# Attention and mixture of experts in one kernel: the tail keys' value product made full-height and rounded

## The chip, the cores and the metric

The kernel runs on one core of a Trainium2 chip. The time is that of one execution on the device, in microseconds (us); before the change it was 874.48 us, the median of three runs (874.23 to 874.96). Smaller is better.

## What is computed

```python
def _attn_ref(q, k, v):                       # 8 x 8 x 576 x 64
    scores = scale * np.matmul(q, k.transpose(0, 1, 3, 2))
    mask = block_i >= block_j                 # blocks of 64 positions
    scores = np.where(mask, scores, -1000000000.0)
    scores = scores - np.max(scores, axis=-1, keepdims=True)
    attn = np.exp(scores)
    attn = attn / (np.sum(attn, axis=-1, keepdims=True) + 1e-09)
    return np.matmul(attn, v)
...
def _moe_ref(x, modality_id, w_gate, modality_bias, w1, w2):   # 4608 x 512, 8 experts
    logits = x @ w_gate + modality_bias[modality_id]
    e_idx = np.argmax(logits, axis=1)
    ...
        h = np.maximum(x[mask] @ w1[e], 0.0)
        out[mask] = gate_w[mask, None] * (h @ w2[e])
```

Attention with a block-causal mask over 64 heads of 576 positions; then each position goes through one of eight experts. The change concerns the last step of the attention, the product of the exponentials with the values, for the last 64 keys and the last 64 queries of each head (576 is four chunks of 128 and a tail of 64).

## The kernel before

**Numbers as head and remainder.** Most products are made from rounded float32 (float32r, fp32r in the profile). A value is split into a rounded head, made by ScalarE (ACT), and a remainder, made by a subtraction on VectorE (DVE) or GpSimd (POOL), which is stored rounded as well. The values of a pair of heads stand in the tile vhl, 8 blocks of 128 keys, with head and remainder side by side as 128 weight columns (64 + 64); the exponentials, transposed, stand in two tiles, pth (heads) and ptl (remainders). A value product is a pair of matmuls with the same weights, one on pth, one on ptl. The output has 128 rows, of which the next product (back, L397) adds the two halves.

**The tail before the change.** The 64 x 64 block of the last keys and last queries goes another way: TensorE transposes the exponentials into 64 rows (L324), ACT copies them to p4 as unrounded float32 (copies, L341), and TensorE multiplies them with the unrounded values in vrt, weights of 64 x 64 (L380, issued at L383). The profile shows an unrounded product as two passes. It is the last product of part "Y", four 320-column ones being ahead of it, and it adds into 64 columns of the accumulator o1 of its head. Part "W", later, adds the other four products into the same accumulator: key chunk 3's (256 columns, two), then key chunk 2's (320 columns, two). "X" fills the first half of the output in another bank.

**The order of the work.** There are 32 pairs of heads. A slot (run_slot, L654) runs the steps of the table ORDER (L49): those with stage 0 for the slot's own pair, those with stage 1 for the pair before. Names: S scores, M maxima, E exponentials, T transposes, C copies to the rounded head (ACT), D remainders (DVE, rests), X, Y, W the value products, x, y their evacuation, K and Z the product back and the output rows; A and B are the two heads, q stands for a step of the routing of an earlier batch. The tail's block is transposed in TA1 and evacuated in CA1 and DA1, late in a pair's own slot; the products YA, WA, YB and WB follow in the next slot. "vh" (split_v) splits the pair's values early in its slot. At a slot's start the inputs of later pairs are loaded (load, L162; load_v, L226) and the next pair's keys and queries are split by POOL (split_qk, L198: L202, L203, L205, L207), with copies inside the chip between partition halves on SP's queue (L196, k2t; L206, z).

**Queues.** Engines TensorE, ACT, DVE and POOL take their work in the program's order throughout. SyncE (SP), which issues most transfers, does so in the first four slots only (L704 to L715); from then on the planner places SP's transfers by its own estimate of when each is ready, and each is then issued in the order it was placed, waiting for its data. The exponentials' four buffers, two pairs by two parts, and the value tiles alternate from pair to pair; vrt has three buffers and is reloaded (L229) when its readers, TensorE's product of the tail among them, are done.

After the attention, from about 440 us, the experts run (class Experts); they share the engines and reuse the buffers of the attention, and nothing of the change stands in them.

Of the kernel before, what the change touches and what calls it, by code (L numbers as in the profile page):

```python
# [11 lines left out]
F32 = mybir.dt.float32  # L12
F32R = mybir.dt.float32r
# [3 lines left out]
ALU = mybir.AluOpType  # L17
# [7 lines left out]
NPAIR = B * H // 2  # L25
# [67 lines left out]
def attention_moe(ctx, tc, qk, vr, bkw, mid, mb, w1, w2, cf, ci, cm, ld, out):  # L93
    nc = tc.nc
    pe, act, dve, pool = nc.tensor, nc.scalar, nc.vector, nc.gpsimd
# [8 lines left out]
    for n, shape in PARTS:  # L104
        size = int(np.prod(shape))
        v = cft[:, off : off + size]
# [21 lines left out]
    att = att_stack.enter_context(tc.tile_pool(name="att", bufs=2, side="right"))  # L128
# [30 lines left out]
    pairs = [Pair() for _ in range(NPAIR)]  # L159
# [66 lines left out]
    def load_v(p):  # L226
        d = pairs[p]
        d.vr = att.tile([128, 640], F32, name="vrt", bufs=3)
        nc.sync.dma_start(d.vr, vr[p])  # L229
        d.v = att.tile([128, 8, 2, 64], F32R, name="vhl", bufs=2)  # L230

    def split_v(p):
        d = pairs[p]
        v8 = d.vr[:, 0:512].rearrange("p (a b) -> p a b", a=8)
        act.copy(d.v[:, :, 0], v8)
        pool.tensor_tensor(d.v[:, :, 1], v8, d.v[:, :, 0], ALU.subtract)

    def scores(p, u):
        d = pairs[p]
# [52 lines left out]
    def row(j):  # L292
        return ROW0 + ROWS[j] * STEP

    def transposes(p, u):
        d = pairs[p]
        t = ps_t.tile([128, 512], F32, name="t")
        ev = []
        if u == "tl":
            for j in range(4):  # L300
                r = ROWS[j]
                pe.transpose(t[:, 128 * r : 128 * r + 128], d.ptail[:, 128 * j : 128 * j + 128], idf)
            src = t.rearrange("p (r h c) -> p h r c", r=4, h=2)
            ev.append((src, [x[:, :, ROW0 : ROW0 + 4 * STEP].rearrange("p h (r c) -> p h r c", r=4)[:, :, :, 256:320] for x in d.pt]))
            d.copies[u] = ev
            return
        h = "AB".index(u[0])
        pm = d.pm[h]

        def blk(c, j):  # L310
            o = CHUNK_OFF[c] + 128 * j
            return pm[:, o : o + 128]

        if u[1] == "0":
            for i, c in enumerate((2, 3, 0, 1)):
                pe.transpose(t[:, 128 * i : 128 * i + 128], blk(c, 0), idf)  # L316
            src = t.rearrange("p (a b) -> p a b", a=2)
            ev.append((src, [two(x, h) for x in d.pt]))
        elif u[1] == "1":
            for i, c in enumerate((1, 2, 3)):  # L320
                pe.transpose(t[:, 128 * i : 128 * i + 128], blk(c, 1), idf)
            ev.append((t[:, 0:384], [x[:, h, 128:512] for x in d.pt]))
            if h == 0:
                pe.transpose(t[0:64, 384:512], d.ptail[:, 512:576], idf)  # L324
                d.p4 = att.tile([64, 128], F32, name="p4", bufs=3)
                ev.append((t[0:64, 384:512], [d.p4]))
        else:
            for i, c in enumerate((2, 3)):
                pe.transpose(t[:, 128 * i : 128 * i + 128], blk(c, 2), idf)
            pe.transpose(t[:, 256:384], blk(3, 3), idf)  # L330
            ev.append((t[:, 0:256], [x[:, h, row(2) : row(2) + 256] for x in d.pt]))
            ev.append((t[:, 256:384], [x[:, h, row(3) + 128 : row(3) + 256] for x in d.pt]))
        d.copies[u] = ev

    def two(x, h):
        v = x[:, h, row(0) - 64 : X0 + 256]
        return v.rearrange("p (a b) -> p a b", a=2)[:, :, 64:320]
# [4 lines left out]

    def rests(p, u):
        for s, dst in pairs[p].copies[u]:
            if len(dst) > 1:
                dve.tensor_tensor(dst[1], s, dst[0], ALU.subtract)  # L346

    def sums(p):
        d = pairs[p]
# [11 lines left out]
    def values(p, h, part):  # L361
        d = pairs[p]
        if part == "X":
            d.o[h, 0] = o0
        if part == "Y":
            d.o[h, 1] = ps_o.tile([128, 512], F32, name="o1")
        mm = []
        for j in range(4):
            for x in d.pt:
                w = d.v[:, 4 * h + j].rearrange("p a b -> p (a b)")  # L370
                if part == "X":
                    if j < 2:
                        a = X0 if j == 0 else 0
                        mm.append((d.o[h, 0][:, 0:256], w, x[:, h, a : a + 256]))
                elif j < 3:
                    mm.append((d.o[h, 1][:, 0:320], w, x[:, h, row(j) : row(j) + 320]))
                else:
                    mm.append((d.o[h, 1][:, 64:320], w, x[:, h, row(j) + 64 : row(j) + 320]))
        if part != "X":
            last = (d.o[h, 1][0:64, 256:320], d.vr[0:64, 512 + 64 * h : 576 + 64 * h], d.p4[:, 64 * h : 64 * h + 64])  # L380
            mm = mm[0:4] + [last] if part == "Y" else mm[6:8] + mm[4:6]
        for i, (o, w, r) in enumerate(mm):
            pe.matmul(o, w, r, start=part != "W" and i == 0, stop=part != "Y" and i == len(mm) - 1)  # L383

# [629 lines left out]
def _constants():  # L1014
    p, j = np.indices((128, 128))
    late = np.arange(128) < 64
    ranks = np.broadcast_to(np.arange(NE) - NE, (128, 5, NE))
    seen = ranks.copy()
    seen[late, 4] = 100
    inv = np.zeros((128, 5))  # L1020
    inv[late, 4] = BIG
    first = np.ones((128, NE, 5))
    first[:, :, 0] = 0
    con = dict(
        idf=p == j,
        ii=p % 64 == j % 64,
        hm=p[:, 0:2] // 64 == j[:, 0:2],
        iom8=ranks[:, 0],
        iom40=ranks,
        iov40=seen,  # L1030
        inv5=inv,
        first5=first,
        base8=np.broadcast_to(np.arange(NE) * REGION, (128, NE)),
        edges=np.broadcast_to(np.arange(N // SLOT) * SLOT, (128, N // SLOT)),
    )
    cf = np.concatenate([con[n].reshape(128, -1) for n, _ in PARTS], axis=1).astype(np.float32)
    at = np.array([0, 128, 256, 384, 448])
    ci = (np.arange(B)[:, None] * S + at)[:, None] + np.arange(128)[None, :, None]
    ci = np.repeat(ci[..., None], IW, axis=3)
    cm = np.zeros((4, 2176), np.float32)  # L1040
    for r in range(4):
        cm[r, 0:1024].reshape(2, 512)[:] = (np.arange(512) >= 128 * r) & (np.arange(512) < 128 * r + 64)
        cm[r, 1024:2176].reshape(2, S)[:] = np.where((np.arange(S) >= 128 * r + 64) & (np.arange(S) < 128 * r + 128), FAR, 0)
    return dict(cf=cf, ci=ci.reshape(B, 128, 5 * IW).astype(np.int32), cm=cm, ld=np.where(j <= p, -1, 0).astype(np.float32))


def _prepare(q, k, v, moe_modality_id, moe_w_gate, moe_modality_bias, moe_w1, moe_w2):
    qt = q.reshape(NPAIR, 2, S, D).transpose(0, 1, 3, 2)
    kt = k.reshape(NPAIR, 2, S, D).transpose(0, 1, 3, 2)
    vp = v.reshape(NPAIR, 2, S, D)  # L1050
    qp = np.zeros((NPAIR, D, 2, 640), q.dtype)
    qp[:, :, 0, 0:576] = qt[:, 0]
    qp[:, :, 1, 0:512] = qt[:, 1, :, 0:512]
    qp[:, :, 1, 576:640] = qt[:, 1, :, 512:576]
    kp = kt.transpose(0, 2, 1, 3).reshape(NPAIR, D, 2 * S)
    qp = qp.reshape(NPAIR, D, 1280)
    one = np.concatenate([qp, kp], axis=2)
    qk = np.concatenate([np.concatenate([one, qp[:, :, 640 * h + 512 : 640 * h + 640]], axis=2) for h in range(2)], axis=1)
    vr = np.zeros((NPAIR, 128, 640), v.dtype)
    vr[:, :, 0:512] = vp[:, :, 0:512].reshape(NPAIR, 2, 4, 128, D).transpose(0, 3, 1, 2, 4).reshape(NPAIR, 128, 512)  # L1060
    vr[:, 0:64, 512:640] = vp[:, :, 512:576].transpose(0, 2, 1, 3).reshape(NPAIR, 64, 128)
    g = moe_w_gate.reshape(H, D, NE).transpose(1, 0, 2)
    bkw = np.zeros((2, D, PPB, 80), moe_w_gate.dtype)
    bkw[:, :, :, 0:8] = g[:, 0::2]
    bkw[:, :, :, 8:72] = np.eye(D)[:, None, :]
    bkw[:, :, :, 72:80] = g[:, 1::2]
    ids = moe_modality_id.reshape(B, S)
    mid = np.zeros((128, B, 5), ids.dtype)
    mid[:, :, 0:4] = ids[:, 0:512].reshape(B, 4, 128).transpose(2, 0, 1)
    mid[:, :, 4] = np.tile(ids[:, 512:576].transpose(1, 0), (2, 1))  # L1070
    mb = np.broadcast_to(moe_modality_bias.reshape(1, 2 * NE), (128, 2 * NE))
    arrays = dict(qk=qk, vr=vr, bkw=bkw.reshape(128, PPB * 80), mid=mid.reshape(128, B * 5), mb=mb, w1=moe_w1, w2=moe_w2, **_constants())
    return {n: np.ascontiguousarray(a) for n, a in arrays.items()}
# [11 lines left out]
```

## Time and profile before

| | |
|---|---|
| median of three runs | 874.48 us (874.23 to 874.96) |
| the profiled execution | 876.53 us, span 874.8 us |
| attention, and experts | about 0 to 440 us, and 440 to 874 us |
| granted TensorE clock over the span | 0.984 |

The profile is that of one execution. Its times are counted from the start of its span; a group of instructions is shown with its line, engine, operation, the tile it writes and those it reads, shapes and count, then its busy time in us, the mean of one in ns, and the idle time of its engine ahead of it with what ended that. PE is TensorE's stream of products, PEld its weight loads, which run beside the products. Products overlap in the records: what one takes of the engine is the distance from its start to the next one's. In the timeline, rows of the same kind are merged with a count; a bracket holds idle time ahead of the row and what released it. SPq rows are issues on SP's queue, not the transfers themselves.

### The profile page before, as it was taken

The page shows a single profiled execution, that of the slowest core. Times are in us where ns is not written, and L with a number is a line of the kernel's source. Part 1 is how long each engine was busy: PE and PEld are TensorE (multiplying, and loading weights), DVE is VectorE, ACT ScalarE, POOL GpSimd, SP SyncE. Part 2 cuts the span into 40 slices and gives each one's busy share as a digit, 9 for nine tenths or more (in the row PEclk, how much of TensorE's full clock was granted, in tenths as well). Part 3 has the DMA queues.
Part 4 walks back from the last instruction along what each step waited for, and adds up shares of the span by engine and source line. Part 5 has one row for each costly group of instructions (what it writes and reads, how often), then busy time and mean ns, then how long its engine had stood idle before and what let it go on. Part 6 is the DMA issues. An engine that isn't in the chain of part 4 may idle for free. (4 is left out here: it accounts for less than half of the span.)

```text
span 874.8 us, 16656 instructions
## 1 busy us (share of the span) xinstructions
PE 844.5 (97%) x5816; PEld 769.4 (88%) x5816; DVE 456.6 (52%) x1653; ACT 457.0 (52%) x1366; POOL 443.6 (51%) x300
## 2 busy tenths in 40 slices
PE   6999999999999999999999999999999999999995
PEld 4889989999998998889889999999999999999884
DVE  6788888888888888878662111111111222222120
ACT  6868888888888888878422222222222222222220
POOL 1967778888797878886855222222211111111100
PEclk7989999999999999999999999999999999999998
DMA  6868666656666585758862121112212222210100
GB/s 187 250 216 245 191 207 203 214 174 230 207 184 201 184 253 141 227 162 222 257 204 76 61 73 73 63 72 73 73 49 73 73 74 73 73 61 25 35 18 18
DMA packets 58183, 120.20 MB, mean 137 GB/s; under 512 B 13458, under 2 KB 24530, under 8 KB 58088
## 3 DMA queue, kind: packets, MB, share of 16 engines
q1 hardware_dynamic: 47344, 95.31, 35.5%
q0 software_dynamic: 10752, 23.79, 8.4%
q8 instruction: 48, 0.79, 0.4%
q14 instruction: 39, 0.32, 0.1%
HBM read 80.12 MB, written 22.25 MB: 117 GB/s over the span
## 5 line engine op out<-in xcount | busy, mean ns | idle before, releaser
L346 DVE TENSOR_TENSOR ptl<-t,pth 128x512 fp32r<-128x512 f32 (+3 forms) x288 | 139.7, 504 | 17.0 <-ACT pth L341 15.4
L341 ACT CAST pth<-t 128x512 fp32r<-128x512 f32 (+3 forms) x288 | 122.0, 451 | 43.6 <-PE t L316 28.9
L290 ACT ACTIVATE pm<-s,nm 128x256 f32<-128x256 f32 (+3 forms) x256 | 134.8, 533 | 14.7 <-DVE scratch L264 14.3
L264 DVE TENSOR_SCALAR_CACHE_REDUCE scratch<-s 128x128 bf16<-128x128 f32 (+4 forms) x288 | 133.0, 479 | 13.3 <-PE s L252 6.7
L383 PE MATMUL o<-pth,vhl 128*128 128x256 f32 (+1 forms) x384 | 114.5, 316 | 6.9 <-DVE o L444 2.4
L918 ACT ACTIVATE scratch<-o,gw 128x512 f32<-128x512 f32 x37 | 25.4, 688 | 172.4 <-PE o L916 101.4
L877 DVE SCALAR_TENSOR_TENSOR qkt<-s,qkt 128x512 fp32r<-128x512 f32 x18 | 12.4, 688 | 189.9 <-ACT qkt L876 189.9
L203 POOL TENSOR_TENSOR z<-raw,qkt 64x1152 fp32r<-64x1152 f32 x30 | 79.5, 2650 | 59.5 <-issue 33.7
L383 PE MATMUL o<-ptl,vhl 128*128 128x256 f32 (+1 forms) x384 | 108.2, 294 | 0.0
L919 POOL DMA_INDIRECT out<-scratch,ids_b x17 | 16.9, 994 | 162.7 <-ACT scratch L918 162.7
L259 PE MATMUL s<-qkt 128*128 128x256 f32 (+2 forms) x256 | 90.5, 364 | 2.6 <-DVE qkt L219 2.6
L870 PE MATMUL s<-z,qkt 128*128 128x256 f32 x720 | 90.2, 283 | 1.3 <-DVE z L856 1.3
L870 PE MATMUL s<-z,w0hb 128*128 128x256 f32 x512 | 91.2, 281 | 0.0
L870 PEld LDWEIGHTS s<-z,qkt 128*128 128x128 f32 x720 | 88.5, 192 | 2.2 <-DVE z L856 1.5
L207 POOL TENSOR_TENSOR qkt<-rawq,qkt 64x1280 fp32r<-64x1280 f32 x30 | 87.9, 2931 | 2.4
L383 PEld LDWEIGHTS o<-pth,vhl 128*128 128x128 f32 x384 | 72.4, 189 | 12.6 <-POOL z L203 9.0
L260 PE MATMUL s<-z 68*128 68x256 f32 (+2 forms) x256 | 81.3, 333 | 0.0
L870 PEld LDWEIGHTS s<-z,w0hb 128*128 128x128 f32 x512 | 79.1, 188 | 0.6
L383 PEld LDWEIGHTS o<-ptl,vhl 128*128 128x128 f32 x384 | 72.9, 190 | 1.4
L870 PE MATMUL s<-z,w0lb 128*128 128x256 f32 x256 | 71.9, 281 | 0.0
L402 PE MATMUL b<-bk,ot 128*128 128x72 f32 x512 | 65.5, 271 | 2.0 <-ACT pth L341 1.2
L402 PEld LDWEIGHTS b<-bk,ot 128*128 128x128 f32 x512 | 65.1, 194 | 2.4 <-ACT pth L341 1.4
(255 smaller groups left out, 1930.2 us busy)
## 6 DMA issues: line engine op xcount, KB each, us to landing
raw<-qk SPq DMA_DIRECT2D x30, 640.0 KB, 6.3
rawq<-qk SPq DMA_DIRECT2D x30, 640.0 KB, 3.8
raw<-w SPq DMA_DIRECT2D x23, 512.0 KB, 3.6
vrt<-vr SPq DMA_DIRECT2D x32, 320.0 KB, 4.4
k2t<-z SPq DMA_DIRECT2D x64, 144.0 KB, 2.4
xrows<-xr SPq DMA_DIRECT2D x8, 1056.0 KB, 9.2
z<-qkt SPq DMA_DIRECT2D x30, 256.0 KB, 4.3
idlist<-btmp SPq DMA_DIRECT2D x8, 304.0 KB, 6.0
```

What stands on the lines that cost most here:

```text
L203: pool.tensor_tensor(d.k2[0:64], k, d.k[0:64], ALU.subtract)
L207: pool.tensor_tensor(d.q[0:64], q, d.q[0:64], ALU.subtract)
L259: pe.matmul(o, d.q[:, h, qs], d.k[:, h, 0:n], start=True, stop=False)
L260: pe.matmul(o, d.q2[0:68, h, qs], d.k2[0:68, h, 0:n], start=False, stop=True)
L264: dve.tensor_scalar(jks[jturn[0] % 4][:, 0 : s.shape[-1]], s, -SCALE, start, ALU.mult, ALU.min, accum_out=o)
L290: act.activation(d.pm[h][:, CHUNK_OFF[c] : CHUNK_OFF[c] + n], s[:, 256 * i : 256 * i + n], AF.Exp, bias=d.nm[:, h, c : c + 1], scale=SCALE ...
L341: act.copy(dst[0], s)
L346: dve.tensor_tensor(dst[1], s, dst[0], ALU.subtract)
L383: pe.matmul(o, w, r, start=part != "W" and i == 0, stop=part != "Y" and i == len(mm) - 1)
L402: pe.matmul(d.b[h][:, 72 * c : 72 * c + 72], d.ot[h][:, 128 * c : 128 * c + 128], w, start=True, stop=True)
L870: nc.tensor.matmul(hp[:, a, :], w[:, kc, ms], x[:, kc, :], start=i == 0, stop=i == len(mm) - 1)
L918: nc.scalar.mul(yo, y, s.gw[:, i : i + 1])
```

## The change

The tail's values are split like all others: the tile vhl gets two more blocks, one for each head. The 64 tail keys stand in it twice, in rows 0 to 63 and again in rows 64 to 127 (the host writes them twice; the bytes loaded stay the same, since those rows held zeros). The transposed exponentials of the tail become a rounded head in rows 0 to 63 of p4 (ACT) and a remainder in p4l (DVE, one new subtraction of 64 x 128 a pair), and SP copies p4l into rows 64 to 127 of p4, one new transfer of 32 KB a pair. One rounded product with 128 x 128 weights and 64 columns then takes the place of the unrounded 64 x 64 one, and it moves from the end of part "Y" to part "W", between the two 320-column products there.

```diff
-        d.v = att.tile([128, 8, 2, 64], F32R, name="vhl", bufs=2)
+        d.v = att.tile([128, 10, 2, 64], F32R, name="vhl", bufs=2)
...
-        v8 = d.vr[:, 0:512].rearrange("p (a b) -> p a b", a=8)
-        act.copy(d.v[:, :, 0], v8)
-        pool.tensor_tensor(d.v[:, :, 1], v8, d.v[:, :, 0], ALU.subtract)
+        v = d.vr.rearrange("p (a b) -> p a b", a=10)
+        act.copy(d.v[:, :, 0], v)
+        pool.tensor_tensor(d.v[:, :, 1], v, d.v[:, :, 0], ALU.subtract)
...
-                d.p4 = att.tile([64, 128], F32, name="p4", bufs=3)
-                ev.append((t[0:64, 384:512], [d.p4]))
+                d.p4 = att.tile([128, 128], F32R, name="p4", bufs=3)
+                d.p4l = att.tile([64, 128], F32R, name="p4l", bufs=2)
+                ev.append((t[0:64, 384:512], [d.p4[0:64], d.p4l]))
...
-            if len(dst) > 1:
-                dve.tensor_tensor(dst[1], s, dst[0], ALU.subtract)
+            dve.tensor_tensor(dst[1], s, dst[0], ALU.subtract)
+        if u == "A1":
+            d = pairs[p]
+            nc.sync.dma_start(d.p4[64:128].bitcast(F32), d.p4l.bitcast(F32))
...
-            last = (d.o[h, 1][0:64, 256:320], d.vr[0:64, 512 + 64 * h : 576 + 64 * h], d.p4[:, 64 * h : 64 * h + 64])
-            mm = mm[0:4] + [last] if part == "Y" else mm[6:8] + mm[4:6]
+            last = (d.o[h, 1][:, 256:320], d.v[:, 8 + h].rearrange("p a b -> p (a b)"), d.p4[:, 64 * h : 64 * h + 64])
+            mm = mm[0:4] if part == "Y" else mm[6:8] + [mm[4], last, mm[5]]
...
-    vr[:, 0:64, 512:640] = vp[:, :, 512:576].transpose(0, 2, 1, 3).reshape(NPAIR, 64, 128)
+    vr[:, :, 512:640] = np.tile(vp[:, :, 512:576].transpose(0, 2, 1, 3).reshape(NPAIR, 64, 128), (1, 2, 1))
```

## Prediction

> **What bounds the kernel.** I read the page first, then the stages, then the timeline of TensorE over two steady slots, and last the queues on which the new copy would stand. Stages first; after the window come busy time (and count) of each engine, granted clock, DMA share and GB/s.
>
> ```profile
> PE 844.5 (97%) x5816; PEld 769.4 (88%) x5816; DVE 456.6 (52%) x1653; ACT 457.0 (52%) x1366; POOL 443.6 (51%) x300
> ...
> core 0: us, PE busy (x) PEld busy (x) DVE busy (x) ACT busy (x) POOL busy (x), PEclk, DMA share, GB/s
> ...
> 25.00:51.00 26.00, 23.83 (x170) 22.02 (x170) 21.98 (x73) 19.71 (x69) 20.85 (x13) 0.94 0.78 253
> ...
> 201.00:251.00 50.00, 49.29 (x377) 45.68 (x376) 42.49 (x180) 43.18 (x150) 41.82 (x26) 1.00 0.65 201
> ...
> 351.00:401.00 50.00, 46.77 (x353) 43.02 (x352) 42.02 (x192) 40.64 (x140) 42.43 (x26) 1.00 0.63 183
> ...
> 440.00:500.00 60.00, 60.00 (x376) 53.59 (x376) 21.27 (x61) 13.84 (x23) 28.08 (x23) 1.00 0.36 119
> ```
>
> In the attention stage TensorE is busy 49.29 of 50 us at the full clock; DVE, ACT and POOL stand at 85, 86 and 84%. From 440 us on (the experts) nothing of the change runs. So a microsecond taken from TensorE in the attention comes off the time, as long as the other three keep up and no new wait is put on TensorE. Two stages are weaker: 25 to 51 us, and 351 to 401 us, where TensorE already idles 3.2 us of 50.
>
> **What the small product costs now.** The timeline of TensorE, one head after the other. Columns: start, time, then line, operation, tiles, array tile, shape.
>
> ```profile
> 202.19 1.01 PE L402 MATMUL b<-bk,ot 128*128 128x72 f32 x8
> 203.04 0.39 PE L404 MATMUL b<-bk,ott 128*128 128x80 f32 x2
> ...
> 206.18 0.31 PE L383 MATMUL o<-ptl,vhl 128*128 128x320 f32 x1
> 206.42 0.33 PE L383 MATMUL o<-p,vrt 64*64 64x64 f32 x2
> 206.68 0.55 PE L321 MATMUL t<-cf,pm 128*128 128x128 f32 x3
> ...
> 207.85 0.31 PE L383 MATMUL o<-ptl,vhl 128*128 128x320 f32 x1
> 207.99 0.39 PE L259 MATMUL s<-qkt 128*128 128x512 f32 x1
> ...
> 211.98 0.30 PE L383 MATMUL o<-ptl,vhl 128*128 128x320 f32 x1
> 212.22 0.33 PE L383 MATMUL o<-p,vrt 64*64 64x64 f32 x2
> 212.47 0.66 PE L316 MATMUL t<-cf,pm 128*128 128x128 f32 x4
> ```
>
> Durations overlap, so I count from start to start. A 320-column product hands over to the next after 0.14 us (207.85 to 207.99). With the small product behind it, the next line starts 0.50 us later in head A (206.18 to 206.68) and 0.49 in head B (211.98 to 212.47). The small product, two passes, thus costs 0.495 − 0.14 = 0.355 us of TensorE, far more than its 64 columns: 0.10 of it is the late start (0.24 instead of 0.14 after the product ahead), the rest two passes of about 0.13. The groups by form say that this is the rule and not these two slots:
>
> ```profile
> L383 PE MATMUL o<-p,vrt 64*64 64x64 f32 x128 | 20.8, 242 | 0.0
> ...
> L383 PEld LDWEIGHTS o<-p,vrt 64*64 64x64 f32 x128 | 12.0, 131 | 12.2 <-issue 11.6 <-DMA k2t<-z 0.2 <-DMA xrows<-wt 0.2
> ```
>
> 128 passes are 64 products, and the weight load idles 12.2 us before them, 0.19 each, for nothing that another engine does: these weights are not loaded while the product ahead runs. In total 64 × 0.355 = 22.7 us.
>
> The Trainium skill, TensorEngine Tiling, Key Properties, says that a change of the tiling mode, not only of the tile, drains TensorE. By that the whole late start goes with the 64*64 tile, as the sum below has it; the 128*64 transposes of this kernel (L324), which the rule would drain too, start without a gap here, so the trace bears it out for the half-height tile alone.
>
> **What it costs after.** One rounded product: 128 x 128 weights, 64 columns, between two products of the same 128*128 form. The trace has no rounded product under 256 columns, so I bound it. Below: 64 of 320 columns at 0.145 us is 0.03. Above: it costs what a 320-column one does, 0.145. The nearest row is L402: 72 columns behind 128 x 128 weights, eight passes in 203.04 − 202.19 = 0.85 us, 0.106 each, which their weight loads set. The new product needs such weights too, and the product behind it loads its own again; I take 0.107. Saved: 0.355 − 0.107 = 0.248 a head, 0.50 a pair, 64 × 0.248 = 15.9 us; with the bounds 13.4 to 20.8.
>
> The Trainium skill, TensorE: Matmul & The Clock Gate, LDWEIGHTS, gives a weight load as its columns over 1.2, in ns, whatever the rows. By that two loads of 64 columns take as long as one of 128, 107 ns (an estimate from that page), so that only the late start would be saved, 64 × 0.10 = 6.4 us. The trace does not agree: the two passes take 0.255 us here, more than such loads would explain, and the measurement decides.
>
> **What the other engines get.** Rows by form, and POOL in one slot:
>
> ```profile
> L236 POOL TENSOR_TENSOR vhl<-vrt,vhl 128x512 fp32r<-128x512 f32 x32 | 40.8, 1275 | 0.1
> ...
> L235 ACT CAST vhl<-vrt 128x512 fp32r<-128x512 f32 x32 | 20.2, 633 | 0.0
> ...
> L346 DVE TENSOR_TENSOR ptl<-t,pth 128x128 fp32r<-128x128 f32 x64 | 17.9, 280 | 0.0
> ...
> 211.77 1.26 POOL L202 CAST qkt<-raw 128x1280 fp32r<-128x1280 f32 x1
> 214.74 2.65 POOL L203 TENSOR_TENSOR z<-raw,qkt 64x1152 fp32r<-64x1152 f32 x1 [1.71 <-issue]
> ```
>
> split_v grows from 512 to 640 columns: ACT 633 × 1.25, so +0.16 us a pair; POOL 1275 × 1.25, +0.32. DVE gets one subtraction of 64 x 128, bounded by the 280 ns of the 128 x 128 row. A slot is 50/4 = 12.5 us and becomes 12.0; in it DVE has 42.49/4 + 0.28 = 10.9 us of work (91%), ACT 43.18/4 + 0.16 = 11.0 (91%), POOL 41.82/4 + 0.32 = 10.8 (90%). POOL's surplus is covered by its wait ahead of L203, 1.71 us here; that wait is for TensorE's last scores of the pair, which come earlier by 0.50 a slot, so 0.9 us of cover is left. ACT's and DVE's hold only on average: between a transpose and its evacuation there are stretches without spare. I charge 1 us over the attention for it, 1 us for the stretch 351 to 401 us, where DVE's routing steps hold TensorE and DVE now has 0.28 more a slot, and 0.5 us for the first three slots. If the cover were gone, the price is 0.28 us a slot, 9 us. The casting of the 64 x 128 block on ACT stays what it was. The loads keep their size; the buffer of vrt comes free earlier, since TensorE no longer reads it, so L229 waits less.
>
> **The new copy.** This is the doubtful part. The remainder is made by DVE at the end of a slot and copied by SP's queue into rows 64 to 127; TensorE needs it in head A's W, third-last of its products there.
>
> ```profile
> 214.26 0.34 PE L260 MATMUL s<-z 68*128 68x384 f32 x1
> ...
> 220.16 0.28 PE L383 MATMUL o<-pth,vhl 128*128 128x256 f32 x1
> 220.28 0.28 PE L383 MATMUL o<-ptl,vhl 128*128 128x256 f32 x1
> 220.40 0.31 PE L383 MATMUL o<-pth,vhl 128*128 128x320 f32 x1
> 220.55 0.31 PE L383 MATMUL o<-ptl,vhl 128*128 128x320 f32 x1
> ...
> 215.12 0.55 DVE L346 TENSOR_TENSOR ptl<-t,pth 128x384 fp32r<-128x384 f32 x1
> ...
> k2t<-z SPq DMA_DIRECT2D x64, 144.0 KB, 2.4
> ...
> 217.42 1.11 SPq L196 DMA_DIRECT2D k2t<-z  x2
> 218.64 0.62 SPq L206 DMA_DIRECT2D z<-qkt  x1
> ```
>
> DVE is done with the remainder at 215.12 + 0.55 + 0.28 = 215.95. A copy inside the chip lands 2.4 us after its issue (k2t, the nearest row, of a larger size), so at 218.4. TensorE comes to the product where its fourth one of W now starts, 220.55, less the 0.355 that Y lost: 220.2. It lands 1.8 us ahead, and the cover is 1.8 us, if SP issues it when DVE is done. Behind it on SP stand the k2t copies, which themselves wait for L203 until 214.74 + 2.65 = 217.39: nothing is held up. But SP's order is not the program's after the first four slots, and here is what it does with a transfer that waits for DVE:
>
> ```profile
> 205.18 1.30 SPq L196 DMA_DIRECT2D k2t<-z  x2
> 206.59 0.53 SPq L507 DMA_DIRECT2D xrows<-xr  x1
> ...
> 202.91 0.55 DVE L346 TENSOR_TENSOR ptl<-t,pth 128x384 fp32r<-128x384 f32 x1
> ...
> 204.20 0.23 DVE L505 RECIPROCAL wt<-o 128x16 f32<-128x16 f32 x1
> ```
>
> L507's data are there at 204.43, and it stands behind both k2t copies, which wait for POOL. The copy's data would come in this slot at 202.91 + 0.55 + 0.28 = 203.74, 0.7 us before L507's, so I take it to be put ahead of the k2t copies or, next likely, between them.
>
> **Sum.** 15.9 − 2.5 = 13.4, say 13 us. The profiled execution took 876.53 us (span 874.8 and 1.7 around it), 2.05 over the median 874.48 of the three runs. 876.53 − 13 = 863.5; on the median that is 861.5.
>
> **Rivals.**
> Slower: the copy is queued too late. If it stands behind both k2t copies, it is issued at 217.42 + 1.11 = 218.53 and lands at 220.9; TensorE waits 0.7 us in each slot, and with 0.50 saved the slot grows by 0.2: 28 slots, +6 us, 880. Behind L206 as well: issue at 219.26, landing 221.7, wait 1.5, +1.0 a slot, 902. It decides from an issue later than 220.7 − 2.4 = 218.3 on. For it speaks L507's place; against it that the copy is ready before L507. Chance 0.16.
> Partly hidden: between the two k2t copies, issued at about 217.97 and landing at 220.4, the copy costs 0.2 a slot, 5.6 us: 867. Or the late start of 0.10 us is not the tile's but the wait's for a late operand, which the new product keeps: 64 × 0.10 = 6.4 us, 868. For the second speaks that the trace names no releaser for that idle time; against it that all 64 have it, in head B too, whose operand is there long before. Chance of either 0.20.
> The product is no cheaper: rounded products of few columns could take several passes, as the unrounded ones do. Then 0.355 stays, and the work on the other engines hides: 874. Nothing shows it, and 256 rounded columns need just 0.12 us (220.16 to 220.28). With it I count the case that ACT or DVE, at 91%, eat the gain. Chance 0.09.
>
> **How the numbers follow.** Forecast 0.55, with a range of its own of 857 to 865 from the bounds on the product's cost and on the losses. A measurement of this kernel tells some 0.2% (1.7 us) from no change. Faster: forecast and the partly hidden, 0.75; within 0.2%: 0.09; slower 0.16. From 857 to 874 lies all but the slower rival and a little below: 8 in 10.
>
> **What would show it.** Right: 64 products of 128 x 64 with 0.11 us to the next start; the last 320-column product of Y hands over in 0.14; a 50 us window of the attention holds more than four slots (12.0 us each) and TensorE still above 97%; the copy on SP between the load of vrt and the k2t copies. Wrong: idle time of TensorE in W put down to the copy, or a queue with the copy behind L196 or L206; idle time ahead of transposes put down to DVE's remainders; 0.24 us ahead of the new product. The experts' 435 us must not change; if they do, the cause is none of the above.

## The result, and the profile after

The change made the kernel slower: 888.6 us, the median of four runs (884.67 to 890.23), beside 874.72 us for the kernel before in the same session (874.23 to 877.68). The ratio is 1.0148, with a 95% interval of 1.0125 to 1.0171. The profiled execution took 887.18 us with a span of 885.5 us, 10.7 over the span of before. The traces are read for these 10.7; the medians lie 13.9 apart, since the profiled run of after is 1.4 us under its median and that of before 1.8 over its own. In the changed kernel the lines behind the edits have moved: the evacuation copies are L342, the copy inside the chip is L349, the value products are issued at L386, and the product back is L405 and L407.

The same views as before: the page's first rows, then the stages (window, length, busy time and count of PE, PEld, DVE, ACT, POOL, granted clock, DMA share, GB/s).

```profile
PE 841.1 (95%) x5752; PEld 777.8 (88%) x5752; DVE 456.2 (52%) x1685; ACT 459.9 (52%) x1366; POOL 452.0 (51%) x300
...
25.00:51.00 26.00, 23.30 (x151) 21.72 (x150) 19.98 (x72) 17.66 (x61) 21.64 (x12) 0.83 0.74 230
201.00:251.00 50.00, 48.48 (x376) 46.49 (x375) 43.85 (x188) 44.28 (x154) 44.26 (x26) 1.00 0.68 215
351.00:401.00 50.00, 45.01 (x316) 42.16 (x314) 40.08 (x188) 37.95 (x129) 40.45 (x25) 0.93 0.53 154
401.00:440.00 39.00, 32.00 (x214) 30.55 (x214) 20.39 (x78) 21.13 (x70) 27.20 (x22) 0.82 0.82 236
440.00:500.00 60.00, 59.17 (x408) 54.72 (x407) 22.73 (x72) 14.39 (x28) 28.17 (x23) 1.00 0.36 115
```

And a stage of before that the prediction does not show:

```profile
401.00:440.00 39.00, 37.70 (x301) 35.84 (x300) 29.50 (x91) 23.56 (x79) 29.07 (x25) 1.00 0.87 254
```

TensorE is now less busy in every stage of the attention. In the steady window that is mild (48.48 of 50 instead of 49.29). In the last 39 us it is not: 32.00 instead of 37.70, at a granted clock of 0.82 instead of 1.00.

**The product itself is as cheap as forecast.** TensorE over the same steady stretch, and two rows of DVE:

```profile
205.85 0.31 PE L386 MATMUL o<-ptl,vhl 128*128 128x320 f32 x1
205.99 0.49 PE L321 MATMUL t<-cf,pm 128*128 128x128 f32 x3
...
212.63 0.31 PE L386 MATMUL o<-pth,vhl 128*128 128x320 f32 x1
212.78 0.19 PE L386 MATMUL o<-p,vhl 128*128 128x64 f32 x1
212.81 0.39 PE L386 MATMUL o<-ptl,vhl 128*128 128x320 f32 x1
213.04 0.49 PE L321 MATMUL t<-cf,pm 128*128 128x128 f32 x3
...
217.05 0.35 PE L386 MATMUL o<-pth,vhl 128*128 128x256 f32 x1 [0.37 <-DVE o L531]
...
214.98 0.27 DVE L346 TENSOR_TENSOR p4l<-t,p 64x128 fp32r<-64x128 f32 x1
...
216.70 0.20 DVE L531 TENSOR_REDUCE o<-o 128x5 f32<-128x40 f32 x1
```

The last product of Y hands over in 0.14 us (205.85 to 205.99), so the late start went with the 64*64 tile. The new product hands over in 0.03 (212.78 to 212.81), and the 320-column product behind it takes 0.23 instead of 0.145, perhaps since its weight load has less to run beside, which is not shown. Together that is 0.115 us a head, where the old one took 0.355. The old product cost a little more than that: the three transposes behind it took 0.55 us (206.68, in the prediction), and now, behind a rounded product, they take 0.49 (205.99). Over the 36 heads between 100 and 330 us the first transpose behind the old product hands over in 0.167 us (median), in the changed kernel in 0.109. With these 0.06 the change takes 0.30 us a head off TensorE, 0.60 a slot; the start-to-start times of pairs 4 to 25 give 0.58.

The groups by form, for what the change added; after the bar come busy time, the mean of one in ns, and idle time ahead:

```profile
L236 POOL TENSOR_TENSOR vhl<-vrt,vhl 128x640 fp32r<-128x640 f32 x32 | 49.6, 1549 | 0.1
L235 ACT CAST vhl<-vrt 128x640 fp32r<-128x640 f32 x32 | 23.8, 743 | 0.0
L386 PE MATMUL o<-p,vhl 128*128 128x64 f32 x64 | 13.9, 217 | 11.7 <-DMA p<-p4l 11.4
L346 DVE TENSOR_TENSOR p4l<-t,p 64x128 fp32r<-64x128 f32 x32 | 8.7, 273 | 0.0
```

The surplus on the other engines is what was forecast or a little less: POOL 0.27 us a pair, ACT 0.11, DVE 0.27. Of the 11.7 us that TensorE idles ahead of the product, 11.4 are the copy's.

**TensorE waits for the copy.** Waits by line and releaser: us in total, times, longest.

```profile
PEld o L386 <- DMA p<-p4l: 14.3, 11, 4.7
PE o L386 <- DMA p<-p4l: 11.4, 6, 4.4
```

A wait shows at the weight load and, where it is longer than the load's lead, at the product as well, so the two rows tell of the same waits and are not added up: TensorE's products waited 11.4 us in 6 places. Between 100 and 330 us lies 0.2 us of it, in one place. The others are in pairs 2 (1.87 us), 26 (2.12), 27 (0.20), 30 (4.45) and 31 (2.56); here are pairs 26 and 30 in the timeline of TensorE, SP and POOL's issues, and SP's issue for pair 31:

```profile
357.38 0.30 PE L386 MATMUL o<-p,vhl 128*128 128x64 f32 x1 [2.12 <-DMA p<-p4l]
359.39 1.96 PE L405 MATMUL b<-bk,ot 128*128 128x72 f32 x8 [0.70 <-DVE b L89]
...
416.36 0.42 PE L386 MATMUL o<-p,vhl 128*128 128x64 f32 x1 [4.45 <-DMA p<-p4l]
418.50 1.82 PE L405 MATMUL b<-bk,ot 128*128 128x72 f32 x8
...
346.87 0.55 SPq L229 DMA_DIRECT2D vrt<-vr  x1
...
352.63 1.11 SPq L196 DMA_DIRECT2D k2t<-z  x2
353.83 0.63 SPq L349 DMA_DIRECT2D p<-p4l  x1
...
408.57 0.38 SPq L812 DMA_DIRECT2D raw<-w  x1
409.04 0.47 SPq L349 DMA_DIRECT2D p<-p4l  x1
...
427.82 0.47 SPq L349 DMA_DIRECT2D p<-p4l  x1
...
408.49 0.80 POOL L816 DMA_DIRECT2D qkt<-w  x1
409.29 0.76 POOL L816 DMA_DIRECT2D z<-w  x1
```

In pair 26 DVE is done at 351.07, SP issues the copy behind both k2t copies at 353.83, and it is waited for until 357.33, 3.5 us later. No load stands right ahead of it on the queue, but an earlier one is still moving: by the transfer packets of the trace some 75 KB of the values' load that SP issued at 346.87 move after 353.83, and both k2t copies too. In the steady slots nothing of that load is left when the copy goes out between the k2t copies. In pair 30 DVE is done at 407.71; SP's queue first holds a load of an expert's weights until that load's buffer is free (408.57); the copy goes out at 409.04, behind this load and a weight transfer from POOL (408.49), with another following (409.29), and lands 7.3 us after its issue. In pair 31 SP is free: DVE is done at 427.74 and the copy goes out at 427.82, but, with a weight load from POOL (426.94) and one from SP (427.11) issued just before it, it lands some 5 us later. In most of the steady slots it lands after 1.9 us. There it goes out as soon as DVE is done, ahead of the k2t copies, or some 2 us later, between them; in the second place it lands just in time, mostly 0.0 to 0.6 us ahead of the product.

**The clock can fall with such a wait.** Granted clock is the third number from the right; the first row begins with the product of pair 26, the third with that of pair 30.

```profile
357.50:366.00 8.50, 7.80 (x35) 7.23 (x36) 4.49 (x21) 4.35 (x16) 4.05 (x4) 0.60 0.58 199
366.00:375.00 9.00, 8.52 (x65) 7.91 (x63) 7.58 (x39) 7.71 (x26) 6.83 (x4) 0.99 0.26 60
416.30:424.00 7.70, 7.64 (x31) 7.15 (x32) 3.13 (x12) 4.21 (x15) 7.21 (x5) 0.50 0.32 106
```

The eight products of L405 take 1.82 and 1.96 us there, and 1.01 at the full clock. Pair 26 lasts 18.1 us instead of 13.5, and pair 30 lasts 20.0 instead of 12.1. The wait and the clock account for it: 8.5 us at 0.60 are 3.4 us lost, 5.5 with the wait of 2.1, and 7.7 us at 0.50 are 3.9, 8.3 with the wait of 4.45; the product's 0.6 a slot comes off both. The Trainium skill, TensorE: Matmul & The Clock Gate, Part 1, has the clock halved after at least one idle window of about 3.4 us; the trace agrees on the halving, but here an unbroken idle time of 2.1 us was followed by it. A wait of that length does not always bring it. In the traces of all kernels here, from 50 to 440 us, half clock came with all ten unbroken waits of 2.5 us or more, and with six of the ten of 1.6 to 2.2 us: the change with q7 later (below) waits 1.99 us in pair 2 and keeps 1.00.

**Where the 10.7 us went.** The time between the starts of the pairs' last products (the first L404 or L407 of each pair) tells the length of each stretch. The table holds, for the profiled execution of each kernel, the length less that of before; the kernels other than the changed one come below.

| kernel | pair 0 | 1 to 3 | 4 to 25 | 26 | 27 to 29 | 30 | 31 | experts | span |
|---|---|---|---|---|---|---|---|---|---|
| the change | +3.5 | 0.0 | −7.7 | +4.6 | −1.0 | +7.9 | +2.2 | +1.2 | +10.7 |
| no copy | +2.1 | −4.3 | −3.6 | +0.6 | −0.8 | +1.9 | −1.5 | +1.0 | −4.5 |
| middle pairs only | +0.1 | −2.9 | −7.2 | 0.0 | 0.0 | 0.0 | +0.3 | +2.0 | −7.7 |
| end pairs only | +1.5 | −0.8 | −1.0 | +4.8 | −1.4 | +7.6 | +0.3 | +1.1 | +12.1 |
| copy in the middle only | +3.0 | −4.3 | −4.1 | +1.7 | −0.8 | +1.4 | −1.5 | +0.9 | −3.6 |
| copy from ACT | +1.0 | −1.1 | −5.2 | +0.6 | −1.1 | −0.1 | +5.4 | +2.0 | +1.5 |
| product alone | +0.5 | −4.6 | −12.7 | +1.3 | −1.7 | −0.6 | +3.9 | −0.1 | −14.0 |
| surplus alone | +2.5 | −4.0 | +2.2 | +0.2 | +0.2 | +0.2 | +6.4 | +1.4 | +9.2 |
| no copy, q7 later | +3.1 | −3.2 | −12.4 | +2.0 | −1.8 | +1.9 | −0.6 | +1.1 | −9.8 |
| before, q7 later | +1.4 | −3.7 | −8.8 | +0.2 | −1.4 | 0.0 | +9.0 | +1.0 | −2.3 |
| the change, q7 later | +1.1 | −2.4 | −9.8 | +0.6 | −1.2 | +9.9 | +6.5 | +1.2 | +5.9 |
| middle, ACT, q7 later | +1.7 | −4.0 | −5.2 | 0.0 | 0.0 | 0.0 | 0.0 | +0.6 | −6.8 |
| middle, no copy, q7 later | +1.1 | −3.7 | −12.6 | 0.0 | 0.0 | 0.0 | +4.4 | −0.1 | −10.9 |

So the change earns 0.35 us in each of the 22 slots of the middle and loses 14.7 us in three pairs at the end (26, 30 and 31). Pairs 0 to 3 differ by a few us between kernels that have nothing in common there; no cause is read from those two columns. Part of it lies in before itself: its profiled run has a clock of 0.50 from 47.9 to 54.7 us, in pairs 1 to 3, which is some 3 us lost, and most of the others have 1.00 there.

### The profile page after: what moved, and what is told of

It is laid out like the page before. It is cut to its first block, busy times and chain, and to the rows that moved or that the text cites. A ratio compares the mean times of both kernels' runs of the same rounds, so it can differ in the third digit from the quotient of the medians.

```text
span 885.5 us, 16620 instructions
## 1 busy us (share of the span) xinstructions
PE 841.1 (95%) x5752; PEld 777.8 (88%) x5752; DVE 456.2 (52%) x1685; ACT 459.9 (52%) x1366; POOL 452.0 (51%) x300
## 5 line engine op out<-in xcount | busy, mean ns | idle before, releaser
L342 ACT CAST pth<-t 128x512 fp32r<-128x512 f32 (+3 forms) x288 | 122.6, 453 | 32.5 <-PE t L316 16.0
L386 PE MATMUL o<-pth,vhl 128*128 128x256 f32 (+1 forms) x384 | 117.7, 324 | 9.4 <-DVE o L447 2.7
L386 PE MATMUL o<-ptl,vhl 128*128 128x256 f32 (+1 forms) x384 | 117.6, 316 | 0.0
L880 DVE SCALAR_TENSOR_TENSOR qkt<-s,qkt 128x512 fp32r<-128x512 f32 x18 | 12.4, 688 | 190.9 <-ACT qkt L879 190.9
L259 PE MATMUL s<-qkt 128*128 128x256 f32 (+2 forms) x256 | 92.3, 370 | 4.0 <-DVE qkt L219 4.0
L386 PEld LDWEIGHTS o<-pth,vhl 128*128 128x128 f32 x384 | 75.2, 196 | 16.7 <-POOL z L203 12.4
L260 PE MATMUL s<-z 68*128 68x256 f32 (+2 forms) x256 | 83.3, 340 | 0.0
L386 PEld LDWEIGHTS o<-ptl,vhl 128*128 128x128 f32 x384 | 75.3, 196 | 1.6
L405 PE MATMUL b<-bk,ot 128*128 128x72 f32 x512 | 66.4, 274 | 1.3 <-DVE b L89 0.7
L405 PEld LDWEIGHTS b<-bk,ot 128*128 128x128 f32 x512 | 65.9, 196 | 1.7 <-ACT ptail L283 1.7
```

The costliest lines, as they stand in the source:

```text
L259: pe.matmul(o, d.q[:, h, qs], d.k[:, h, 0:n], start=True, stop=False)
L260: pe.matmul(o, d.q2[0:68, h, qs], d.k2[0:68, h, 0:n], start=False, stop=True)
L342: act.copy(dst[0], s)
L405: pe.matmul(d.b[h][:, 72 * c : 72 * c + 72], d.ot[h][:, 128 * c : 128 * c + 128], w, start=True, stop=True)
```

## The experiments

The theory was: the copy is late where SP issues it behind loads, and the half clock doubles what that costs. The rivals were: the surplus on DVE, ACT and POOL costs the time; the new product is not cheaper after all. Each run was timed beside the kernel before on the same chip.

**Without the copy.** POOL doubles the tail's 64 exponentials, the transpose then gives 128 rows, ACT rounds all of them, and DVE subtracts in place in rows 64 to 127.

```diff
+            if i == 1:
+                pool.tensor_copy(d.ptail[:, 576:640], d.ptail[:, 512:576])
...
-                pe.transpose(t[0:64, 384:512], d.ptail[:, 512:576], idf)
+                pe.transpose(t[:, 384:512], d.ptail[:, 512:640], idf)
...
+                ev.append((t[:, 384:512], [d.p4]))
...
+                dve.tensor_tensor(dst[0][64:128], s[64:128], dst[0][64:128], ALU.subtract)
...
-            nc.sync.dma_start(d.p4[64:128].bitcast(F32), d.p4l.bitcast(F32))
```

> The copy on SP's queue is taken out and all else kept: POOL doubles the tail's 64 columns of exponentials (128 x 64) ahead of the transpose, the transpose gives 128 rows, ACT rounds all of them into p4, and DVE makes the remainder in rows 64 to 127 in place. Theory C (the copy: it lands late for pairs 0, 2, 26, 30 and 31, each wait is some 2 to 5 us and is followed by half clock; all other slots gain 0.34 us): 32 x 0.34 = 11 us faster than before, 862 to 866. Theory S (the surplus on DVE, ACT and POOL is what is late, and the copy only shows it): the surplus is all here, so still 880 or more.

Measured: 875.28 us beside 875.3, ratio 1.000 (0.9988 to 1.0012), between the spans of both theories. The loss is gone, but no gain came in its place; the profiled run, 872.0, is the fastest of this kernel's runs, so its row in the table flatters it. Pair 26 keeps the full clock:

```profile
201.00:251.00 50.00, 47.84 (x371) 45.71 (x369) 44.73 (x189) 44.29 (x150) 44.12 (x30) 1.00 0.66 203
351.00:401.00 50.00, 45.32 (x346) 43.15 (x347) 44.40 (x202) 41.30 (x142) 41.78 (x30) 1.00 0.61 165
...
212.92 0.60 PE L318 MATMUL t<-cf,pm 128*128 128x128 f32 x4
214.19 0.38 PE L387 MATMUL o<-pth,vhl 128*128 128x256 f32 x1 [0.66 <-DVE o L532]
...
213.93 0.20 DVE L532 TENSOR_REDUCE o<-o 128x5 f32<-128x40 f32 x1
```

The steady stretch shows a second loss that has nothing to do with the copy. TensorE, busy 47.84 of 50 us, waits ahead of the first product of X for a DVE reduction of the routing (step q7). That step leaves its results in o, in the half of the accumulator into which X multiplies next. Added up from start to start between 100 and 330 us, what this step takes beyond its usual length is 4.2 us before, 7.7 after the change and 12.2 here; with the surplus alone (below) it is 5.8 and with the product alone 5.6. DVE, with more to do, comes to q7 later, while TensorE comes to X earlier.

**The change in the middle pairs only, and in the end pairs only.** Pairs 4 to 23 have the new product and the others the old one; then the other way round (the text behind # in the first line is the other run's range).

```diff
+NEW = range(4, 24)            # the end pairs: (0, 1, 2, 3, *range(24, NPAIR))
...
+                if p in NEW:
                     d.p4 = att.tile([128, 128], F32R, name="p4", bufs=3)
...
+            if p in NEW:
                 mm = mm[0:4] if part == "Y" else mm[6:8] + [mm[4], last, mm[5]]
```

> The change as it is, copy included, for pairs 4 to 23 alone; all others as before. Theory C: 20 slots gain 0.34 each and none of the late copies is there: 867 to 869. Theory S says the same where the surplus does not bite, that is up to 874.

> The complement: the change for pairs 0 to 3 and 24 to 31, all others as before. Theory C: the late copies are all here and few slots gain: 889 to 897, slower than the whole change. If the loss were spread over all slots, 12 of 32 slots would give 12/32 of it: 879.

Measured: the middle alone 868.46 us, ratio 0.9918 (0.9901 to 0.9934); the ends alone 890.32, ratio 1.0186 (1.0155 to 1.0217). The same edit is faster in one place and slower in the other, and the table shows the whole change's gain of the middle in the one and its losses of pairs 26 and 30 in the other. The totals do not add up, though: −6.8 and +15.0 make +8.2, not 13.9. The traces put most of the rest into pairs 0 to 3, from which no cause is read.

**The copy in the middle pairs only.** All pairs have the new product; pairs 0 to 3 and 24 to 31 make the remainder without a copy.

```diff
+NOCOPY = (0, 1, 2, 3, *range(24, NPAIR))
...
-        if u == "A1":
+        if u == "A1" and p not in NOCOPY:
             d = pairs[p]
             nc.sync.dma_start(d.p4[64:128].bitcast(F32), d.p4l.bitcast(F32))
```

> The changed kernel with the new product in all pairs; the copy on SP's queue stays in pairs 4 to 23, and pairs 0 to 3 and 24 to 31 make the remainder without a copy (POOL doubles the tail's 64 columns, the transpose gives 128 rows, DVE subtracts in place). Copies that land late behind loads are the cause of the loss at both ends: that loss goes, pair 26 takes 13.5 to 15 us instead of 18.1, pair 30 12 to 14 instead of 20.0, and the middle keeps its 0.35 us a slot; median 867 to 871 beside some 875. The surplus work of the engines, or the product's later place, is the cause: the ends stay slow, pairs 26 and 30 above 17 us, median 882 or more, as with the change in the end pairs alone (890).

Measured: 872.03 us beside 875.04, ratio 0.9964 (0.9940 to 0.9987), 1 us above the span given. Pair 26 took 15.2 us and pair 30 took 13.5, where they had taken 18.1 and 20.0: the copy, and not the surplus or the product's later place, cost most of the time at the end. Against before, 1.7 and 1.4 us stay. The missing microseconds are the same fault in a new place. Pair 4, the first with a copy, came directly behind two loads:

```profile
73.82 1.11 SPq L183 DMA_DIRECT2D raw<-qk  x1
75.03 0.93 SPq L232 DMA_DIRECT2D vrt<-vr  x1
76.40 0.49 SPq L363 DMA_DIRECT2D p<-p4l  x1
...
82.95 0.30 PE L400 MATMUL o<-p,vhl 128*128 128x64 f32 x1 [1.82 <-DMA p<-p4l]
84.10 1.31 PE L419 MATMUL b<-bk,ot 128*128 128x72 f32 x8
86.15 1.05 PE L307 MATMUL t<-cf,ptail 128*128 128x128 f32 x4
```

The copy of 32 KB, issued at 76.40, is waited for until 82.9, 6.5 us. Four transposes then take 1.05 us instead of 0.60, and the slot takes 16.2 us, where it took 12.5 in the changed kernel.

**The copy from ACT's queue.**

```diff
-            nc.sync.dma_start(d.p4[64:128].bitcast(F32), d.p4l.bitcast(F32))
+            act.dma_start(d.p4[64:128].bitcast(F32), d.p4l.bitcast(F32))
```

> The whole change, but the copy is issued by ACT, in the program's order, as soon as DVE has made the remainder, not by SP. If the place in SP's queue is what makes it late (behind a 512 or 640 KB load issued just ahead, behind the k2t copies): the waits of 2 to 5 us and the half clock after them go, all slots gain, 864 to 869, if ACT's waiting for DVE costs nothing. If a copy lands late in these stretches from whatever queue, since the transfers' engines are full: 880 to 888.

Measured: 878.45 us beside 875.61, ratio 1.0040 (1.0026 to 1.0053), between the two spans given. The products' waits for the copy fall from 11.4 us to 2.0, and up to pair 30 the trace is 6.0 us ahead of before. Pair 26 shows that queue and transfer engines each had a part: the copy still lands 4.7 us after its issue, but it is issued at 350.59, as soon as DVE is done (350.56), and the product waits 0.28 us. Then pair 31 loses 5.4, by a cause that the run with the surplus alone explains.

**The product alone.** The new product multiplies a constant tile of zeros with the values of key chunk 0; there is no wider split, no subtraction and no copy.

```diff
+    p4s = inp.tile([128, 128], F32R, name="p4s")
+    dve.memset(p4s.bitcast(F32), 0.0)
...
+            last = (d.o[h, 1][:, 256:320], d.v[:, 4 * h].rearrange("p a b -> p (a b)"), p4s[:, 64 * h : 64 * h + 64])
```

> The new product alone, at its new place, on a constant tile of zeros and the weights of key chunk 0, so the tail's keys are left out of the result: no copy, no wider split, no subtraction. By the trace of the change a product takes 0.115 us instead of 0.355: 64 x 0.24 = 15 us under before if nothing else waits, 859 to 861. If X's wait grows as TensorE gets faster (DVE does the same work in a shorter slot), half of that: 866 to 869. The last rows' place in SP's queue can add 6 to 9.

Measured: 863.84 us beside 874.21, ratio 0.9865 (0.9832 to 0.9899), between the spans given. The tail keys are thus missing from its output. Its middle gains 12.7 us in 22 slots, 0.58 each, all of it in the product and the transposes behind it; the prediction had 0.50. This is what the idea is worth when its operands cost nothing. Pair 26 loses 1.3 us here too, to a wait for a copy of ACT, so that stretch is tight without a copy of the remainder; pair 31 loses 3.9, with a wait of 3.7 us of the experts for DVE.

**The surplus alone.** The old product with the wider split and the added subtraction, whose result is not used.

```diff
-        d.v = att.tile([128, 8, 2, 64], F32R, name="vhl", bufs=2)
+        d.v = att.tile([128, 10, 2, 64], F32R, name="vhl", bufs=2)
...
+                d.p4l = att.tile([64, 128], F32, name="p4l", bufs=2)
+                ev.append((t[0:64, 384:512], [d.p4, d.p4l]))
```

> The old product at its old place, with the surplus work alone: the wider split of the values on ACT and POOL and one more subtraction of 64 x 128 on DVE, whose results nobody reads; no copy. Theory C: TensorE is the slower one, most of it hides; at most the longer wait ahead of X, 0.17 us a slot: 874 to 880. Theory S: 882 or more.

Measured: 885.49 us beside 875.3, ratio 1.0113 (1.0096 to 1.0130). Taken by the time alone this would make the surplus the culprit. The table says otherwise: the middle loses 2.2 us (0.10 a slot), and 6.4 of the 9.2 are lost in pair 31. There SP, POOL and TensorE show:

```profile
402.98 7.92 SPq L810 DMA_DIRECT2D raw<-w  x2
410.99 0.46 SPq L508 DMA_DIRECT2D xrows<-xr  x1
411.54 0.52 SPq L513 DMA_DIRECT2D xrows<-wt  x1
...
422.27 1.10 POOL L840 DMA_INDIRECT xr<-xrows,ids_lead  x1 [10.28 <-DVE p4l L347]
...
425.82 0.30 PE L853 MATMUL t<-cf,xr 128*128 128x128 f32 x1 [3.88 <-DMA xr<-xrows,ids_lead]
427.25 0.90 PE L853 MATMUL t<-cf,xr 128*128 128x128 f32 x3 [1.13 <-DMA xr<-xrows,ids_lead]
```

Before, the routing's rows went out at 402.58, right behind the weight load of 402.01. Here the planner put them behind one load more (the second of the x2), which waits for its buffer. They go out at 410.99 and land at 421.3; the gather of POOL, put down to DVE's p4l in the bracket, starts at 422.27, where before it started at 413.22; TensorE waits 5 us for it and then has half the clock (0.52 from 426 to 433 us). The same order shows in three more kernels, the copy from ACT and the two of the next paragraph that come from before and from the change, and costs 5.4 to 9.0 us in their pair 31. It is not in the changed kernel.

**The routing step behind X.** ("q7", 2) moves in ORDER from in front of CB0 to behind ("xA", 1), so that X no longer waits for it: in the kernel without the copy, in the kernel before as the control, and in the changed kernel.

```diff
-    ("SA2", 0), ("CA2", 1), ("vh", 0), ("MA2", 0), ("SA01", 0), ("TB0", 1), ("q7", 2), ("CB0", 1),
+    ("SA2", 0), ("CA2", 1), ("vh", 0), ("MA2", 0), ("SA01", 0), ("TB0", 1), ("CB0", 1),
...
-    ("TB1", 1), ("DB0", 1), ("xA", 1), ("St1", 0), ("r", 1), ("WA", 1), ("CB1", 1), ("Mt1", 0),
+    ("TB1", 1), ("DB0", 1), ("xA", 1), ("q7", 2), ("St1", 0), ("r", 1), ("WA", 1), ("CB1", 1), ("Mt1", 0),
```

> No copy (POOL doubles the columns, as in the run without the copy), and the routing step q7, DVE's last work in the accumulator bank o0 ahead of X of head A, is moved behind x of head A. Theory: X waits for that step, 0.69 us a slot without the copy against 0.36 before; moved away, the wait goes and each slot loses some 0.6: 0.6 x 30 = 18 us under the 875 of the run without the copy, 857 to 861. If X's wait is for POOL's or ACT's surplus, it stays: 873 to 876.

> The kernel before with only the routing step q7 moved behind x of head A, as a control: X's wait there is 4.15 us from 100 to 330 us, 0.23 a slot, so 5 to 8 us less than before, 867 to 870, and not the 18 us of the run without the copy.

> The whole change with q7 moved likewise. X's wait of 7.65 us from 100 to 330 us goes, some 11 us in all; the copy's late landings for pairs 0, 2, 26, 30 and 31 stay, and TensorE comes earlier to the product, so the copy, landing 1.9 us after its issue, is waited for in more slots, 0.2 to 0.4 each: 878 to 884.

Measured: without the copy 866.42 us, ratio 0.9892 (0.9876 to 0.9909); before 873.46, ratio 0.9974 (0.9963 to 0.9985); the change 888.94, ratio 1.0167 (1.0124 to 1.0210), all beside 875.61 and all above the spans given. Without the copy TensorE's steady window is full again:

```profile
201.00:251.00 50.00, 49.67 (x381) 47.17 (x380) 45.21 (x193) 45.25 (x156) 45.52 (x30) 1.00 0.69 211
```

The move takes 8.8 us off the middle of the kernel without the copy (−3.6 to −12.4). The control shows that it is worth 8.8 us in the middle for the kernel before as well, and that only the late rows of pair 31 (+9.0) hide it in the total. So the move did not free a gain that the wait ahead of X had held back: measured against its control, the change without a copy is worth 3.6 us in the middle with q7 at either place. The changed kernel keeps its late copies: its products wait 24.2 us for them, in 14 places, since TensorE now comes to the product earlier in the steady slots too (its profiled run, 882.34, is the fastest of its runs, so its row flatters it).

**Two combinations.** The middle pairs alone with the copy from ACT, and the middle pairs alone without a copy; in both, q7 stands behind X in the slots of the middle, and everything else is as before.

```diff
+NEW = range(4, 24)            # without a copy: range(4, 25)
...
+                if name == ("q7" if 4 <= slot < 25 else "q8"):            # without a copy: slot < 26
+                    continue
```

> What the runs so far point to: the change for pairs 4 to 23 alone, the copy issued by ACT, and the step q7 behind x of head A in slots 4 to 24 alone, so that the order at both ends stays that of the kernel before. Theory (three separate terms: late copies at the ends, X's wait for DVE's routing step, and the planner's order of the last rows behind a weight load): 7 us of the run with the middle pairs plus 0.4 x 20 of X's wait, 15 us under before: 859 to 862. If X's wait only turns into another wait: 866 to 869.

> Pairs 4 to 24 have the new product, made without a copy, and the routing step q7 stands behind xA in slots 4 to 25; all other pairs and slots are as before. If TensorE's wait ahead of X for the routing and the copies at the ends are all that kept the gain away, the slots of the middle take 12.0 us (0.55 less than before), pair 26 stays at 13.5 to 14, the end keeps its 12.1 and 21.4: 861, between 859 and 864. If POOL's or ACT's surplus is what limits the middle, the slots stay at 12.2 or more: 867 to 870.

Measured: with ACT 869.85 us beside 874.21, ratio 0.9951 (0.9932 to 0.9970), a miss; without a copy 864.48 beside 875.04, ratio 0.9867 (0.9826 to 0.9908), just above the span given. With ACT as the issuer the wait only moved:

```profile
211.67 0.47 ACTq L358 DMA_DIRECT2D p<-p4l  x1
212.18 0.58 ACT L294 ACTIVATE pm<-s,nm 128x384 f32<-128x384 f32 x1 [0.82 <-DVE o L537]
...
212.91 0.66 PE L320 MATMUL t<-cf,pm 128*128 128x128 f32 x4 [0.29 <-ACT pm L294]
```

ACT, which issues the copy, stands until DVE has made the remainder; its exponential starts 0.82 us late, and TensorE's transposes wait for it. The version without a copy is the fastest that holds the whole computation. Its middle gains what the product alone gained (12.6 us), but by the control 8.8 of that belong to the moved step and 3.8 to the change. Its pair 31 loses 4.4 us to a wait of the experts for DVE:

```profile
411.49 5.28 PE L891 MATMUL s<-z,qkt 128*128 128x256 f32 x23 [3.08 <-DVE z L877]
```

Why the moved step (8.8) and the product (12.7 alone) do not add up is seen from start to start on TensorE, over pairs 4 to 25. A slot is 12.22 us in the control and 12.04 here. The product and the transposes behind it take 0.58 us off, as they do alone. But X's first product, which follows its transposes in 0.03 us in all 28 places of the control between 100 and 330 us, waits again for DVE's routing, 0.20 us a slot more; the transposes of the tail take 0.13 more, where TensorE waits for POOL to double the columns; and 0.07 lies in the rest. These waits are short, and the busy time hardly shows them: TensorE is busy 49.5 of 50 us there.

## Why the prediction was wrong

**The price of the product: right, and a little low.** 0.115 us a head against 0.107 forecast, so 64 × 0.24 = 15.4 us against 15.9. The 0.06 a head by which the old product delayed the transposes behind it, another 3.7 us in 64 heads, were not in the prediction. The rivals that kept the late start or the passes fell. The estimate that the prediction worked out from the Trainium skill's sentence on weight loads (TensorE: Matmul & The Clock Gate, LDWEIGHTS), 6.4 us saved, is not borne out: 15.4 by these rows, and the product alone gained 12.7 in 22 of the 32 slots.

**The copy: the step that failed.** The prediction said: "A copy inside the chip lands 2.4 us after its issue", and "It lands 1.8 us ahead". In most of the steady slots the landing held, and better (1.9 us). The lead of 1.8 us did not: where the copy stood between the two k2t copies, the place taken as next likely, it mostly landed 0.0 to 0.6 us ahead, and only the shorter landing kept the rival priced at 0.2 us a slot for that place away. The landing failed where loads stood right ahead of the copy or were still moving: 4.9 us from issue to landing in pair 0, 3.8 in pair 2, 3.5 in pair 26, 7.3 in pair 30, some 5 in pair 31. In pair 19, in the middle, it took 4.7 us as well, but there the copy went out as soon as DVE was done, and the product waited 0.2. The price was taken from one steady slot and the median of another transfer and was carried to all 32 pairs. The slower rival named half of the mechanism, a copy queued too late, as in pair 26 behind both k2t copies, but priced it as the same small wait in each of 28 slots. It is a few long waits, and most of them lie between 351 and 440 us, of which the prediction read only the first 50 us, and charged those only with DVE's routing.

**The clock: a term that was missing.** A wait was priced at its length. Pair 26, with a wait of 2.1 us, lost 4.6, and pair 30, with 4.45 us, lost 7.9; with a copy in neither pair, the same product lost 1.7 and 1.4 us there. The trace of before had the warning: its window from 25 to 51 us shows 0.94.

**The other engines: the cover was mis-sized.** Their added work was priced rightly; what it costs was not. "I charge 1 us over the attention". The surplus alone cost 0.10 us a slot, 2.2 us in 22 slots, nearly all of it in a longer wait for the routing ahead of X. In the changed kernel, with TensorE earlier as well, that wait grew by 3.5 us from 100 to 330 us. From start to start over pairs 4 to 25 the product and the transposes behind it give 0.58 us a slot, X's wait takes 0.16 of that and waits for the copy some 0.07, most of them too short for the list of waits: that is why the middle gave 0.35. A charge of 1 us for 351 to 401 us stood against 4.6 in pair 26 alone, most of it by the copy.

**The experts: nearly unchanged**, +1.2 us in a part that the edit does not touch; kernels with quite different edits show −0.1 to +2.0 there. What sets this stays open, as does the start (pair 0), where the prediction had charged 0.5 us for the first three slots.

## What to carry to other kernels

When a change puts a transfer between two engines, price its landing in every stage, behind what its queue and the transfer engines carry there, and not from the steady slot: the steady slots hid this copy, and three pairs at the end lost nearly twice what the 22 of the middle had earned. Allow for a wait of TensorE of about 2 us to cost more than twice its length, since half clock came with more than half of those seen here. Measure an edit against a control that has the other edit alone: moving q7 gave 8.8 us in the middle of the kernel before as in that of the change without a copy. And compare by stretch before blaming an edit by its total: the surplus alone looked 10 us slower, and some two thirds of it was one transfer placed behind another.

## What the runs showed of the hardware

- A rounded product of 64 columns between two of 320, all with 128 x 128 weights, took 0.115 us; the unrounded one of 64 x 64 took 0.355, and the transposes behind it another 0.06.
- A copy of 32 KB inside the chip landed 1.9 us after its issue in most slots, and 3.5 to 7.3 us after it with loads right ahead of it or still moving.
- With an unbroken wait of TensorE of 1.8 us (pair 4 of the copy in the middle only), 2.1 us (pair 26) and 4.45 us (pair 30) the clock was half for some microseconds; a wait of 1.99 us (pair 2 of the change with q7 later) and waits of 0.3 to 1.2 us in each slot, in the kernel without the copy, left it at 1.00.
- One queue's order, changed by a planner in answer to an edit elsewhere, went with 5.4 to 9.0 us more in pair 31 of four kernels.
